# V and wq through GpSimd's DMA queue, and tile 3 of each head transposed by DMA instead of by TensorE

## The chip, the cores and the metric

The kernel runs on one core of a Trainium2 chip. The metric is device time in microseconds (us) of one launch; lower is better. The time before is the median of three runs, and one further execution was recorded by the hardware profiler. The engines are named as in the profile: PE is TensorE (PEld its weight loads), DVE is VectorE, ACT is ScalarE, POOL is GpSimd, SP is SyncE, which only issues DMAs here.

## What is computed

A transformer block: an adaptive layer norm, multi-head attention of 2048 queries against a cached K and V (32 heads of 128, no mask), an output projection, and then a token-shift mixer with an MLP. The change touches the attention alone.

```python
h = _layernorm(x) * (1 + ca) + sa            # x: 1 x 2048 x 640; sa, ca, ... from c and w_mod
q = (h @ wq).reshape(B, Sq, 32, 128).transpose(0, 2, 1, 3)
scores = einsum('bhqd,bhkd->bhqk', q, k_cache) * 128 ** (-0.5)
p = softmax(scores, axis=-1)
o = einsum('bhqk,bhkd->bhqd', p, v_cache)    # k_cache, v_cache: 1 x 32 x 2048 x 128
x = x + ga * (o.transpose(0, 2, 1, 3).reshape(B, Sq, 4096) @ wo)
...                                          # layer norm, mixer and MLP: not touched
```

## The kernel before

**Order of the work.** The program is written as one list of operations for each engine. A small planner (`Prog`) gives each operation the semaphore waits that its reads and writes need; the order on each engine is the order in which the operations are added. A DMA belongs to the queue of the engine that issues it, and waits there like any other operation.

**Attention, step by step.** The loop of line 516 runs over steps s. Step s handles tile j = s % 16 (128 queries) of head h = s // 16, so a head has 16 steps. In each step:

- PE makes the scores of the tile, 128 x 2048 (`qk`, L286), in two halves in PSUM (`Sps`).
- DVE copies each half to SBUF as `negS`, scaled by a negative factor, and takes its minimum in the same instruction (L559). `negS` has three buffers.
- POOL joins the two minima to one (`nm`, L569), and ACT makes the exponentials from `negS` and `nm` (L572) in bf16 into `Pb`, a ring of 8 tiles (`RPB`). So the exponential of tile s writes the place of tile s - 8.
- The tile is transposed, so that keys lie on the partitions: from `Pb` to `PTs`, a ring of 12 tiles. For most tiles a DMA does this on SP's queue (`transpose`, L222), for two neighbouring tiles in one DMA where both go that way. For the tiles in `PE_TILES`, 3 and 10 of each head, PE transposes sixteen 128 x 128 blocks to PSUM three and four steps later (`t_piece`, L253), and ACT (L262) or DVE (L264) copies each half of eight blocks to `PTs` (`t_evac`). DVE copies one half of tile 3 (`by_dve`); ACT copies the other half and both of tile 10.
- PE multiplies the transposed tile of 8 to 11 steps earlier with V (`pv`, L299), ACT copies the result of two tiles to `Of` (L550), and POOL divides by the row sums (L440, L447) and writes four tiles at once to a scratch tensor in DRAM, by a DMA on POOL's own queue (L454).

So with tiles 3 and 10 left out, a head's transposes on SP's queue are the pairs 0-1, 4-5, 6-7, 8-9, 12-13 and 14-15, and tiles 2 and 11 alone: eight DMAs for 14 tiles.

**Loads inside the loop.** All on SP's queue, one head or two ahead, double buffered by head: K of the next head, itself a DMA transpose from DRAM (`load_k`, L205), after step 2; the columns of wq for the head after the next (`load_wq`, L209, 160 KB), after step 6; V of the next head (`load_v`, L214, 512 KB in runs of 256 bytes), after step 12. The projection of the next head's queries is cut into 20 pieces (`q_piece`, L237), which PE runs between the other matmuls in the half steps that `QPIECE` names; it keeps clear of the half steps in which a tile of `PE_TILES` is transposed, since both use the same two PSUM banks. ACT copies each finished 512 columns (L244).

After the last step, the scratch tensor is read back transposed, and the projection, the mixer and the MLP follow.

Of the kernel before, what the change touches and what calls it, by code (L numbers as in the profile page):

```python
# [115 lines left out]
def bass_adaLN_cond__mha_block_cached__mixer_s_mlp__prompt_kernel(  # L116
# [7 lines left out]
    NQT = SQ // 128  # L124
# [13 lines left out]
    with ExitStack() as es:  # L138
# [11 lines left out]
        if True:  # L150
            with ExitStack() as es1:
                sb1 = lambda name, shape, dt: es1.enter_context(nc.sbuf_tensor(name, shape, dt))
                RPB, RPT = 8, 12
                PVD, PVE = 11, 8
                PE_TILES = (3, 10)
                US = KT * (SQ + 4)
                sb1("pad", [128, 32], F32)
                ring = sb1("ring", [128, RPB + RPT, SK], BF16)
# [16 lines left out]
                Vaug = kv[:, o1:o2].rearrange("p (b k d) -> p b k d", b=2, k=NKT)  # L175
                wq = kv[:, o2:o3].rearrange("p (b k d) -> p b k d", b=2, k=KT)
# [24 lines left out]
                G = Prog(nc, es1, "a")  # L201
# [2 lines left out]
                    hb = h % 2  # L204
                    G.dma("sync", lambda e: e.dma_start_transpose(KTs[:, hb], A_k_cache[0, h]), ("k", hb), w=[("KT", hb)])  # L205

                def load_wq(h):
                    hb = h % 2
                    G.dma("sync", lambda e: e.dma_start(wq[:, hb], A_wq[:, h * 128:(h + 1) * 128].rearrange("(k p) d -> p k d", p=128)),  # L209
                          ("wq", hb), w=[("wq", hb)])  # L210

                def load_v(h):
                    hb = h % 2
                    G.dma("sync", lambda e: e.dma_start(Vaug[:, hb, :, 0:128], A_v_cache[0, h].rearrange("(t p) d -> p t d", p=128)),  # L214
                          ("v", hb), w=[("V", hb)])

                assert RPB % 2 == 0 and RPT % 2 == 0 and NQT % 2 == 0
                is_pe = lambda g: g % NQT in PE_TILES

# [14 lines left out]
                def q_piece(h, cc, q):  # L234
                    hb = h % 2
                    jb = bank(("q", h, cc))
                    G.op("tensor", lambda t: t.matmul(JB[jb], wq[:, hb, q, :], hT[:, q, cc * 512:(cc + 1) * 512],  # L237
                                                      start=(q == 0), stop=(q == KT - 1)),
                         r=[("wq", hb), ("hT", cc, q)], w=[("J", jb)])
# [23 lines left out]
                    else:  # L263
                        G.op("vector", lambda v: v.tensor_copy(dst, src), r=[("J", jb)], w=[("PT", g % RPT, r)])  # L264

                by_dve = lambda g, r: r == 1 and g % NQT == PE_TILES[0]

                taken = [u for j in PE_TILES for u in range(2 * (j + 3), 2 * (j + 5))]
                QPIECE = {}
# [62 lines left out]
                if H > 1:  # L332
# [8 lines left out]
                     r=["id0"], w=["ident"])  # L341
# [3 lines left out]
                for k in range(KT):  # L345
                    G.op("gpsimd", lambda g, k=k: g.tensor_scalar(out=s_bc[:, k, :], in0=ones_f, scalar1=c_f[:, k:k + 1],
                                                                  scalar2=1.0, op0=ALU.mult, op1=ALU.mult),
                         r=["onesf", "cf"] + WRK, w=[("sbc", k)])
# [52 lines left out]
                def q_head0(cc):  # L401
                    for q in range(KT):
                        q_piece(0, cc, q)
                    q_evac(0, cc)
# [22 lines left out]
                def mod_rows(i):  # L427
                    n0, n1 = MROW[i]
                    bank = PO[:, (i % 2) * 512:(i % 2) * 512 + n1 - n0]

                    def f(t):
                        for k in range(KT):
                            ins = t.matmul(bank, s_bc[:, k, :], wmodr[:, k, n0:n1], start=(k == 0), stop=(k == KT - 1))
                        return ins
                    G.op("tensor", f, r=[("sbc", k) for k in range(KT)] + [("wm", 1)] + WRK, w=[("O", i % 2)])
                    G.op("scalar", lambda a: a.copy(mod_bc[:, n0:n1], bank), r=[("O", i % 2)], w=[("mod", i)])
# [70 lines left out]
                for g in range(NG):  # L507
                    d = max(PVE, min(PVD, PVE + (NG - 12 - g) // 2))
# [7 lines left out]
                for s in range(at[-1] + LAG + 1):  # L516
                    h, j = divmod(s, NQT)
                    pvs = PVS.get(s, [])
                    evacs = []
                    if s <= 2:  # L520
                        for i in ((0,), (1, 2), range(3, len(MROW)))[s]:
                            mod_rows(i)
                    if s == 3:
                        G.op("gpsimd", lambda g: g.tensor_scalar(
                            out=mod_bc[:, 2 * D:3 * D], in0=mod_bc[:, 2 * D:3 * D], scalar1=1.0, scalar2=1.0, op0=ALU.add, op1=ALU.mult),
                            r=[("mod", i) for i in range(len(MROW))], w=["mod"])
                    for half in range(2):
                        if s < NG:
                            qk(s, half)
                        for g_ in pvs:  # L530
                            if len(pvs) == 1:
                                pv(g_, half)
                            elif g_ == pvs[half]:
                                pv(g_, 0)
                                pv(g_, 1)
                        if s == 0 and half == 1:
                            q_head0(NQC - 1)
                        if h + 1 < H and 2 * j + half in QPIECE:
                            cc, q = QPIECE[2 * j + half]
                            q_piece(h + 1, cc, q)  # L540
                            if q == KT - 1:
                                evacs.append((q_evac, h + 1, cc))
                        for r in range(2):
                            g = s - 3 - r
                            if 0 <= g < NG and is_pe(g):
                                t_piece(g, r, half)
                                if half == 1:
                                    evacs.append((t_evac, g, r))
                    for p in [g_ // 2 for g_ in pvs if g_ % 2 == 1]:
                        G.op("scalar", lambda a, p=p: a.copy(  # L550
                            Of[:, p % 4].rearrange("p z d -> p (z d)")[:, 0:259], PO[:, (p % 2) * 512:(p % 2) * 512 + 259]),
                            r=[("O", p % 2)], w=[("Of", p % 4)])
                    for fn, x, y in evacs:
                        if fn is q_evac or not by_dve(x, y):
                            fn(x, y)
                    for half in range(2):
                        if s < NG:
                            r8 = s % 8
                            G.op("vector", lambda v, half=half, s=s, r8=r8: v.tensor_scalar(  # L559
                                out=negS[:, s % 3, half * 1024:(half + 1) * 1024],  # L560
                                in0=Sps[:, half * 1024:(half + 1) * 1024],
                                scalar1=-SCALE, scalar2=None, op0=ALU.mult, op1=ALU.min,
                                accum_out=(nm0 if half == 0 else nm1)[:, r8:r8 + 1]),
                                r=[("S", half)], w=[("negS", s % 3), ("nmh", half, r8)])
                    for fn, x, y in evacs:
                        if fn is t_evac and by_dve(x, y):
                            fn(x, y)
                    if s < NG:
                        G.op("gpsimd", lambda g, r8=r8: g.tensor_scalar(  # L569
                            out=nm[:, r8:r8 + 1], in0=nm0[:, r8:r8 + 1], scalar1=nm1[:, r8:r8 + 1], scalar2=None, op0=ALU.min),  # L570
                            r=[("nmh", 0, r8), ("nmh", 1, r8)], w=[("nm", r8)])
                        G.op("scalar", lambda a, s=s, r8=r8: a.activation(  # L572
                            Pb[:, s % RPB, :], negS[:, s % 3, :], ACT.Exp, bias=nm[:, r8:r8 + 1], scale=-1.0),
                            r=[("negS", s % 3), ("nm", r8)], w=[("Pb", s % RPB)])
                        if not is_pe(s):
                            if s % 2 == 1 and not is_pe(s - 1):
                                transpose(s - 1, 2)
                            elif s % 2 == 1 or is_pe(s + 1):
                                transpose(s, 1)
                        if j == 2 and h >= 1 and h + 1 < H:  # L580
                            load_k(h + 1)
                        if j == 6 and h + 2 < H:
                            load_wq(h + 2)
                        if j == PVD + 1 and h + 1 < H:
                            load_v(h + 1)
                    for g_ in NORMS.get(s, []):
                        gr, z = divmod(g_, 4)
                        if z == 0:
                            rcp(gr)
                        norm(gr, z)  # L590
                    if s == OT0:
                        load_ot(0)
                        for cc in range(NQC):
                            load_xt(cc)
                    if s == OT0 + 1:
                        load_ot(1)
# [98 lines left out]
                for n in range(KT):  # L695
                    lst = []
                    p = 0
                    while p < 128:
# [8 lines left out]
                        p = pe_  # L707
# [136 lines left out]
```

## Time and profile before

| | |
|---|---|
| Three runs | 1612.88, 1617.95 and 1618.99 us, median 1617.95 us |
| The profiled execution | 1604.1 us, of which its span, from the first to the last instruction, 1602.3 us |
| Granted TensorE clock over the span | 0.993 |
| Attention loop, 37.8 to 1255 us of the span (1217.2 us) | PE busy 1147.1 us, DVE 1192.1, ACT 1194.8, POOL 551.5; DMA moved 240 GB/s |
| The rest, 1255 to 1602.3 us (347.3 us) | PE busy 326.6 us, DVE 173.5, ACT 78.4, POOL 68.5; DMA moved 86 GB/s |
| L559, DVE's scaling with minimum | 1024 times, 1.220 us each |
| L572, ACT's exponentials | 512 times, 2.029 us each |
| L262, ACT's copies of transposed halves | 96 times, 1.034 to 1.042 us each |
| L264, DVE's copies of transposed halves | 32 times, 0.686 us each |
| L253, PE's transposes of blocks | 1024 times, 0.218 us each |
| L222, DMA transposes issued by SP | 256 times, SP's issue 1.63 to 7.63 us, median 4.36; landed 7.1 us after issue in the median |
| L214, loads of V | 32 times, SP's issue 0.58 us in the median; landed after 5.2 us |
| L209, loads of wq | 32 times, SP's issue 0.58 us in the median; landed after 3.6 us |
| L454, results to the scratch tensor, POOL's queue | 128 times, 128 KB each, POOL's issue 0.81 us; landed after 4.5 us |

Busy times are unions of an engine's instructions; a duration of one is longer than the distance between the starts of two in a row where the engine overlaps them. An issue on SP's queue lasts until its descriptors are handed over, and is not a busy time of an engine; the landing is when the last part of the data has arrived. The DMA share of a stretch is the time that packets took on the 16 DMA engines; packets overlap, so it can pass 1, and the bytes moved tell more.

### The profile page before, as it was taken

How to read it: one execution, taken by the hardware profiler on the slowest of the kernel's cores; microseconds unless marked ns; L12 is line 12 of the kernel's file. 1: busy time of each engine (PE TensorE's matmuls, PEld its weight loads, DVE VectorE, ACT ScalarE, POOL GpSimd, SP SyncE). 2: the span in 40 equal slices, each digit the busy share in tenths (PEclk: the TensorE clock that was granted, in tenths of full speed). 3: DMA queues.
4: the chain of work that ended last, by engine and by line, in shares of the span. 5: the costliest groups of instructions: out<-in, count | busy, mean ns of one | idle time of the engine just before them, and what ended most of it. 6: DMA issues, size and time to landing. Idle time of an engine off the chain costs nothing.

```text
span 1602.3 us, 34804 instructions
## 1 busy us (share of the span) xinstructions
PE 1492.6 (93%) x13978; PEld 963.0 (60%) x14231; DVE 1392.5 (87%) x2460; ACT 1288.2 (80%) x1145; POOL 622.8 (39%) x1394
## 2 busy tenths in 40 slices
PE   5799999999999999999999999999999799999998
PEld 3466666666666666666666666666666555545444
DVE  6999999999999999999999999999999266666424
ACT  4999999999999999999999999999999300055330
POOL 0144444444444444444444444444444423322000
PEclk9999999999999999999999999999999899999999
DMA  9999999999999999999999999999999994530000
GB/s 305 229 230 239 238 243 237 253 241 240 237 237 233 239 237 237 239 239 247 243 250 246 250 239 235 246 228 239 236 244 244 241 196 106 106 111 1 17 17 34
DMA packets 1167730, 333.62 MB, mean 208 GB/s; under 512 B 1148304, under 2 KB 1161552, under 8 KB 1167568
## 3 DMA queue, kind: packets, MB, share of 16 engines
q1 hardware_dynamic: 1161424, 314.59, 98.3%
q0 software_dynamic: 6144, 16.79, 3.3%
q8 instruction: 112, 1.84, 0.5%
q14 instruction: 50, 0.41, 0.1%
HBM read 43.48 MB, written 19.40 MB: 39 GB/s over the span
## 4 chain that ended last, share of the span: by engine, by line
DVE 30%; ACT 24%; PE 20%; DMA 15%; issue 10%; POOL 0%; SPq 0%; ACTq 0%; DVEq 0%
DVE negS L559 27%; ACT ring L572 19%; DMA ring<-ring 13%; PE Sps L631 8%; PE Sps L772 4%; PE Oaug L756 2%; PE QPp L756 2%; ACT ring L262 2%; ACT Of L550 2%; PE Sps L741 1%; ACT kv L244 1%; DMA ring<-in_A_x_dram 1%; DVE ring L364 1%; DMA negS<-o_scratch 1%; PE Sps L286 1%
## 5 line engine op out<-in xcount | busy, mean ns | idle before, releaser
L559 DVE TENSOR_SCALAR_CACHE_REDUCE negS<-Sps 128x1024 f32<-128x1024 f32 x1024 | 1177.2, 1220 | 22.2 <-PE Sps L286 12.5
L572 ACT ACTIVATE ring<-negS,small 128x2048 bf16<-128x2048 f32 x512 | 1011.4, 2029 | 21.9 <-DMA ring<-ring 15.7
L299 PEld LDWEIGHTS PTp<-kv,ring 128*128 128x128 bf16 x8192 | 560.0, 98 | 245.0 <-DMA ring<-ring 6.7
L286 PE MATMUL Sps<-kv 128*128 128x512 bf16 x1949 | 596.3, 383 | 62.8 <-DVE negS L559 42.9
L299 PE MATMUL PTp<-kv,ring 128*128 128x129 bf16 x8192 | 645.6, 221 | 6.5 <-DMA ring<-ring 5.6
L569 POOL TENSOR_SCALAR small<-small 128x1 f32<-128x1 f32 x512 | 145.8, 285 | 621.5 <-DVE negS L559 621.4
L286 PEld LDWEIGHTS Sps<-kv 128*128 128x128 bf16 x2048 | 124.5, 97 | 187.2 <-DVE negS L559 158.0
L447 POOL TENSOR_SCALAR On<-Of,small 128x128 bf16<-128x128 f32 x512 | 189.8, 371 | 13.0
L669 ACT COPY kv<-PTp 128x640 bf16<-128x640 bf16 x32 | 22.0, 692 | 155.0 <-PE PTp L666 154.9
L440 POOL TENSOR_TENSOR small<-Of,small 128x4 f32<-128x4 f32 x128 | 133.2, 1040 | 6.3 <-ACT Of L550 6.2
L454 POOL DMA_DIRECT2D o_scratch<-On x128 | 103.1, 806 | 40.8 <-POOL On L447 37.2
L237 PE MATMUL Oaug<-hTx,kv 128*128 128x512 bf16 x265 | 101.2, 387 | 7.9 <-ACT ring L262 4.2
L550 ACT COPY Of<-PTp 128x259 f32<-128x259 f32 x256 | 99.5, 389 | 10.5 <-PE PTp L299 10.5
L237 PE MATMUL QPp<-hTx,kv 128*128 128x512 bf16 x259 | 97.5, 381 | 2.5 <-ACT hTx L391 1.8
L559 DVE DVE_READ_ACCUMULATOR negS<-Sps 128x1 f32 x1024 | 85.4, 83 | 0.0
L612 POOL TENSOR_SCALAR On<-On 128x1 f32<-128x1 f32 x48 | 24.3, 507 | 152.9 <-DVE On L621 152.9
L639 DVE TENSOR_TENSOR ring<-Sps,mod_bc 128x640 f32<-128x640 f32 x16 | 13.2, 825 | 77.0 <-PE Sps L631 77.0
L631 PE MATMUL Sps<-wo,hTx 128*128 128x128 bf16 (+1 forms) x504 | 71.8, 304 | 5.0 <-DMA hTx<-o_scratch 4.7
L776 DVE TENSOR_TENSOR ring<-Sps,ring 128x640 f32<-128x640 f32 x16 | 13.2, 825 | 66.2 <-PE Sps L772 66.2
L631 PE MATMUL Sps<-wo,negS 128*128 128x128 bf16 (+1 forms) x504 | 69.1, 298 | 1.3 <-DMA negS<-o_scratch 0.9
L262 ACT COPY ring<-Oaug 128x1024 bf16<-128x1024 bf16 x64 | 66.2, 1034 | 0.0
L631 PEld LDWEIGHTS Sps<-wo,hTx 128*128 128x128 bf16 x512 | 40.2, 99 | 36.9 <-DMA hTx<-o_scratch 4.5
(82 smaller groups left out, 1011.2 us busy)
## 6 DMA issues: line engine op xcount, KB each, us to landing
kv<-in_A_v_cache_dram SPq DMA_DIRECT2D x32, 512.0 KB, 5.2
o_scratch<-On POOLq DMA_DIRECT2D x128, 128.0 KB, 4.5
ring<-in_A_x_dram SPq DMA_DIRECT2D x8, 640.0 KB, 4.9
kv<-in_A_wq_dram SPq DMA_DIRECT2D x32, 160.0 KB, 3.6
wo<-in_A_wo_dram SPq DMA_DIRECT2D x1, 5120.0 KB, 16.4
ring<-ring SPq DMA_TRANSPOSE x256, 7.1
ring<-in_w_mod_dram SPq DMA_DIRECT2D x1, 3200.0 KB, 13.6
out_dram<-wo SPq DMA_DIRECT2D x16, 160.0 KB, 1.8
```

Source lines behind the costliest of these rows:

```text
L237: G.op("tensor", lambda t: t.matmul(JB[jb], wq[:, hb, q, :], hT[:, q, cc * 512:(cc + 1) * 512], start=(q == 0), stop=(q == KT - 1)), r=[(" ...
L262: G.op("scalar", lambda a: a.copy(dst, src), r=[("J", jb)], w=[("PT", g % RPT, r)])
L286: ins = t.matmul(Sps[:, col:col + 512], QT[:, hb, j * 128:(j + 1) * 128], KTs[:, hb, col:col + 512], start=True, stop=True)
L299: ins = t.matmul(ob[:, 0:129], PTs[:, b, kt, :], Vaug[:, hb, kt, 0:129], start=(kt == 0), stop=(kt == NKT - 1))
L440: G.op("gpsimd", lambda g: g.tensor_tensor(out=rl[:, 4 * b:4 * b + 4], in0=Of[:].rearrange("p a z d -> p (a z) d")[:, 4 * b:4 * b + 4, 128 ...
L447: G.op("gpsimd", lambda g: g.tensor_scalar(out=On[:, b, z, :], in0=Of[:, 2 * b + z // 2, z % 2, 0:128], scalar1=rl[:, 4 * b + z:4 * b + z ...
L454: G.dma("gpsimd", lambda e: e.dma_start(o_scr[jj // 2:jj // 2 + 2, :, hh].rearrange("a p z d -> p a (z d)"), On[:, b].rearrange("p (a z) d ...
L550: G.op("scalar", lambda a, p=p: a.copy(Of[:, p % 4].rearrange("p z d -> p (z d)")[:, 0:259], PO[:, (p % 2) * 512:(p % 2) * 512 + 259]), r= ...
L559: G.op("vector", lambda v, half=half, s=s, r8=r8: v.tensor_scalar(out=negS[:, s % 3, half * 1024:(half + 1) * 1024], in0=Sps[:, half * 102 ...
L569: G.op("gpsimd", lambda g, r8=r8: g.tensor_scalar(out=nm[:, r8:r8 + 1], in0=nm0[:, r8:r8 + 1], scalar1=nm1[:, r8:r8 + 1], scalar2=None, op ...
L572: G.op("scalar", lambda a, s=s, r8=r8: a.activation(Pb[:, s % RPB, :], negS[:, s % 3, :], ACT.Exp, bias=nm[:, r8:r8 + 1], scale=-1.0), r=[ ...
L631: ins = t.matmul(YB[b][:, c0:c0 + cw], OTj[pr % 2][:, 2 * hh + z, :], wo[:, hh, c0:c0 + cw], start=(hh == 0), stop=(hh == H - 1))
```

## The change

`PE_TILES` becomes `(10,)`. Tile 3 is then no longer transposed by PE, and neither ACT nor DVE copies it; it joins tile 2 in one DMA transpose of two tiles on SP's queue. A head's transposes on that queue are still eight, now for 15 tiles. `by_dve` is always false: both halves of tile 10 stay with ACT, as before, and DVE copies none. `QPIECE` now has to keep clear of tile 10's half steps alone, so the 20 pieces fall on half steps 0 to 19 (before: 0 to 9 and 16 to 25).

Inside the loop the loads of wq and of V are issued on POOL's queue, at the same places of the program: behind L569 of step 6 and of step 12, and ahead of the normalization that POOL does in that step. The loads ahead of the loop (wq of heads 0 and 1, V of head 0) and all loads of K stay on SP's queue.

```diff
-                PE_TILES = (3, 10)
+                PE_TILES = (10,)
...
-                def load_wq(h):
+                def load_wq(h, q="sync"):
                     hb = h % 2
-                    G.dma("sync", lambda e: e.dma_start(wq[:, hb], A_wq[:, h * 128:(h + 1) * 128].rearrange("(k p) d -> p k d", p=128)),
-                          ("wq", hb), w=[("wq", hb)])
-
-                def load_v(h):
+                    G.dma(q, lambda e: e.dma_start(wq[:, hb], A_wq[:, h * 128:(h + 1) * 128].rearrange("(k p) d -> p k d", p=128)),
+                          ("wq", hb, q), w=[("wq", hb)])
+
+                def load_v(h, q="sync"):
                     hb = h % 2
-                    G.dma("sync", lambda e: e.dma_start(Vaug[:, hb, :, 0:128], A_v_cache[0, h].rearrange("(t p) d -> p t d", p=128)),
-                          ("v", hb), w=[("V", hb)])
+                    G.dma(q, lambda e: e.dma_start(Vaug[:, hb, :, 0:128], A_v_cache[0, h].rearrange("(t p) d -> p t d", p=128)),
+                          ("v", hb, q), w=[("V", hb)])
...
-                by_dve = lambda g, r: r == 1 and g % NQT == PE_TILES[0]
+                by_dve = lambda g, r: False
...
                         if j == 6 and h + 2 < H:
-                            load_wq(h + 2)
+                            load_wq(h + 2, "gpsimd")
                         if j == PVD + 1 and h + 1 < H:
-                            load_v(h + 1)
+                            load_v(h + 1, "gpsimd")
```

## The prediction

> **What bounds the kernel now.** First the page's busy times and DMA queues.
>
> ```profile
> PE 1492.6 (93%) x13978; PEld 963.0 (60%) x14231; DVE 1392.5 (87%) x2460; ACT 1288.2 (80%) x1145; POOL 622.8 (39%) x1394
> ...
> DMA  9999999999999999999999999999999994530000
> ...
> q1 hardware_dynamic: 1161424, 314.59, 98.3%
> q0 software_dynamic: 6144, 16.79, 3.3%
> ```
>
> In the loop (slices 2 to 32) PE, DVE, ACT and the DMAs all stand at 9. q1 is SP's queue, q0 POOL's. The table by stretches tells DVE and ACT apart from the rest (PE, PEld, DVE, ACT, POOL busy; clock; DMA share; GB/s):
>
> ```profile
> 120.00:320.00 200.00, 192.36 (x1969) 130.32 (x2003) 200.00 (x351) 200.00 (x168) 94.02 (x215) 1.00 1.21 242
> ...
> 520.00:720.00 200.00, 187.00 (x1908) 127.49 (x1942) 194.60 (x340) 194.76 (x163) 90.38 (x209) 1.00 1.24 238
> ```
>
> Early in the loop DVE and ACT never pause. There a head lasts 37.2 us (first L572 of heads 1 to 9, each 37.22 us after the last). That is DVE's work: 32 L559 start 1.144 us apart in the timeline, 36.6 us, and one L264 adds 0.6. Later both lose 5 us in 200, and heads last 37.0 to 39.6 us. The chain of waits in that part names the cause, and the list of waits the same:
>
> ```profile
> 533.09 9.63 DMA ring<-ring
> ...
> 542.80 1.03 ACT ring L572
> 543.83 8.12 DMA ring<-ring
> ...
> 552.03 1.81 ACT ring L572
> ```
>
> ```profile
> ACT ring L572 <- DMA ring<-ring: 15.7, 26, 1.7
> ```
>
> An exponential may not overwrite its place in `Pb` until the DMA has transposed the tile of eight steps before. Now SP's timeline over one head (start, duration, count at the end):
>
> ```profile
> 551.61 2.01 SPq L205 DMA_TRANSPOSE kv<-in_A_k_cache_dram  x1
> 553.66 4.58 SPq L222 DMA_TRANSPOSE ring<-ring  x1
> 558.29 0.59 SPq L209 DMA_DIRECT2D kv<-in_A_wq_dram  x1
> 558.92 11.00 SPq L222 DMA_TRANSPOSE ring<-ring  x3
> 569.96 0.58 SPq L214 DMA_DIRECT2D kv<-in_A_v_cache_dram  x1
> 570.59 19.46 SPq L222 DMA_TRANSPOSE ring<-ring  x4
> 590.10 2.48 SPq L205 DMA_TRANSPOSE kv<-in_A_k_cache_dram  x1
> ```
>
> Each issue starts 0.04 us after the one before: SP's queue never rests. It doesn't wait for ACT either: between 78 and 1216 us (heads 1 to 31) a transpose of tiles 4-5 is issued after its exponentials are done by 1.5 us in head 1, 5.1 in head 4, 7 to 8 in heads 9 to 16. The queue falls behind by 0.6 us a head until the ring of eight is full, and then sets the pace. Its issue times, means of 28 heads between 150 and 1200 us: pairs 0-1, 4-5, 6-7, 8-9, 14-15 take 4.53, 4.54, 4.78, 4.58, 4.49 us; pair 12-13, behind V, 6.27; tiles 2 and 11 alone 2.65 and 2.21; K 2.24, wq 0.59, V 0.58; eleven gaps 0.5. Sum 38.0 us a head. So three limits lie close together: the DMA stream 38.0 us, DVE 37.2, ACT some 37.5 (194.8 busy in 200 us, of a head of 38.5).
>
> **What is removed.** A head of DVE's loses L264, 0.6 us: floor 36.6. ACT's loses one L262, 1.0 us: floor 36.5. PE's loses sixteen L253, four groups of 0.39 us, 1.55 us, from an engine that waits for DVE (158.0 us at L286). None of this is gain while the DMA stream is the longest; it lowers the floor under it, by at most 38.0 - 36.6 = 1.4 us a head. The projection's pieces and ACT's L244 only move.
>
> **What SP's queue loses.** V: its issue with the gap 0.63 us, and the delay of the pair behind it, 6.27 - 4.58 = 1.69; 2.3 together. wq: 0.63 and 4.78 - 4.54 = 0.24, so 0.9. Together 3.2 us a head.
>
> **What it gains.** Tile 2 alone becomes pair 2-3: 4.55 instead of 2.43 (mean of the two single tiles), +2.1 us; at least +1.8, the time of 512 KB at 289 GB/s, the stretch 561 to 564 us in which transposes run undisturbed; at most 4.55 - 2.21 = +2.3. I take 2.0. K of the next head now goes ahead of this pair, whose DMA starts a step later; tile 2 already waits 8.2 us for its issue, so the step is covered.
>
> So SP's queue by itself would need 38.0 - 3.2 + 2.0 = 36.8 us.
>
> **What V and wq cost on POOL's queue.** The trace of before shows none there. Its nearest row is L454, 128 KB four times a head. In windows of 1 to 3 us around its packets:
>
> ```profile
> 561.00:564.00 3.00, 2.85 (x37) 2.24 (x37) 3.00 (x7) 3.00 (x4) 0.62 (x2) 1.00 1.27 289
> 559.00:560.00 1.00, 1.00 (x15) 0.75 (x13) 1.00 (x3) 1.00 (x1) 0.56 (x2) 1.00 0.85 222
> 588.00:590.00 2.00, 2.00 (x23) 1.27 (x21) 2.00 (x5) 1.63 (x2) 0.64 (x2) 1.00 1.27 36
> ```
>
> The first is undisturbed; L454's packets fall at 559.3 us, and just ahead of 588, where the stream then all but stops for two microseconds while its last packet is out. A fit of the distances between landings of the transposes (on tiles, K, wq, V and L454's packets) gives 1.0 us for one L454. Bounds for the 672 KB of V and wq: **from below 0**, if they fit into the stalls that the stream has anyway (38.0 us carry some 31 us of data at 289 GB/s); **from above 5.3 us**, L454's 1.0 us for each 128 KB. Between lie 2.4 us (688 KB in decimal units at 289 GB/s) and 3.2 us, what the same bytes cost now. I take **3.2**, since the same runs of 256 bytes pass the same 16 DMA engines.
>
> The Trainium skill has a rule against the change: "DMA: Bandwidth & Descriptors", section "Issuing engines are not separate DMA queues", says that transfers of SP and POOL run on the same 16 DMA engines, and issuing from both saves only the issuing time. By it the sum below would be +0.7 us a head; that is a rival.
>
> **POOL.** L454 holds POOL 0.81 us for 256 runs. V has 2048 runs, wq 640: between 0.8 us each and 6.4 and 2.0 us by runs. Behind V on POOL stand that step's L447 (0.37) and L569 of step 13, for which the exponential waits; it is due 2.29 us after the last L569 and is used 1.4 us after its end. So up to 3 us are hidden; 6.4 would idle ACT 3.4 us a head. Then ACT needs 36.5 + 3.4 = 39.9 us, still within a head of 40.0, and the ring covers the moment. V and wq wait for nothing: PE has read the old buffers at step 10 and in the head before. They are needed 15 and 10 steps later, 35 and 24 us, against landings of 5.2 and 3.6 us.
>
> **Sum.** 36.8 + 3.2 = 40.0 us a head against 38.0, **+2.0 us**. Head 0 has idle DMA time, so 31 heads: +62 us. The 347 us after the loop stay. The profiled execution's 1602.3 us of span become 1664, its 1604.1 us 1666; the median of the runs shown lies 13.9 us higher (0.9%), so 1617.95 + 62 = **1680 us**.
>
> **Rivals.**
>
> *The loads cost only bytes.* V and wq keep their DMA time, and the stream saves 2 x 0.63 us of issue: -1.26 + 2.0 = +0.7 us a head, +23 us, 1641; with 2.4 us for the loads, 36.8 + 2.4 = 39.2, +37, 1655. For it: V is read, where L454 writes, and what follows a write may not follow a read. Against: SP's issues wait for the DMA engines rather than these for SP, so issue time saved is not stream time saved. This is the skill's rule.
>
> *POOL's packets stop the stream as L454's do.* 36.8 + 5.3 = 42.1, +4.1 us a head, +127 us, 1745. For it: the stall at 588. Against: much of an L454's price may be per transfer and not per byte, and there are two more transfers, not five.
>
> *Faster: the loads fill the stalls.* V and wq use time in which the transposes stand still. Then the stream needs 36.8 us, about DVE's floor, and a head lasts 36.8: -1.2 x 31 = -37, 1581. It decides if the loads cost less than 1.2 us a head (where 36.8 + cost equals 38.0), and POOL is held less than about 4.5 us. For it: 7 us a head of stalls. Against: stalls come mostly beside other transfers, so the loads bring stalls of their own, and 1.2 us is half the time of their bytes.
>
> *The change doesn't do what it says:* no; the planner adds no wait that would put the loads back.
>
> **How the numbers follow.** Chances: forecast (loads at 2.5 to 4.2 us) 0.42, from +1.3 to +3.0 us a head, 1658 to 1711; bytes only, 1626 to 1658, 0.18; as L454, over 1711, 0.13; within 0.5% of 1618 (1610 to 1626, about what a measurement here can tell from no change) 0.08; faster 0.19. The range reaches from 1592, which leaves out the better part of the faster case, to 1735: about 1 in 10 is left out on each side. Faster 0.19, same 0.08, slower 0.73.
>
> **What would show it.** DVE and ACT busy per head down by 0.6 and 1.0 us, but more waits of L572 for the transposes, several times 15.7 us, from head 2 or 3 on. SP's issues still back to back, pair 12-13 down to some 4.6 us, pair 2-3 at 4.5, and pairs near V's packets longer. POOL's instruction for V between 0.8 and 6.4 us. Wrong: SP's queue with pauses and heads of 36.6 to 37 us, or L572 waiting for L569 more than for the DMA.

## The result, and the profile after

The changed kernel takes 1724.89 us (median of four runs, 1716.73 to 1741.2) against 1618.47 us before: a ratio of 1.0676, 95% interval 1.0593 to 1.0758, +106 us by the medians. The forecast was slower, +62 us. The profiled execution took 1723.53 us, its span 1721.7. Runs more than 1.5% above the fastest of the same kernel are left out of the ratios below: two of four with wq back on SP's queue, one of four with wq at step 8.

The page's busy times and DMA queues, after:

```profile
PE 1502.4 (87%) x13474; PEld 943.6 (55%) x13719; DVE 1380.2 (80%) x2428; ACT 1264.8 (73%) x1113; POOL 692.5 (40%) x1455
...
DMA  9999999999999999999999999999999996630000
...
q1 hardware_dynamic: 1143296, 310.19, 93.3%
q0 software_dynamic: 12528, 37.96, 9.4%
```

DVE and ACT have less to do in more time; the DMAs are as full as before, and POOL's queue q0 now carries 38 MB instead of 17. The same two stretches as before (PE, PEld, DVE, ACT, POOL busy; clock; DMA share; GB/s):

```profile
120.00:320.00 200.00, 175.26 (x1707) 114.53 (x1738) 179.61 (x314) 175.90 (x147) 97.51 (x208) 0.99 1.21 233
520.00:720.00 200.00, 169.06 (x1624) 111.22 (x1655) 171.66 (x297) 170.31 (x142) 91.80 (x195) 0.97 1.21 230
```

DVE and ACT, which before never paused early in the loop, now idle 20 to 30 us in 200, and the DMAs move 230 to 233 GB/s, where 238 to 242 were moved before. The waits and a piece of the chain say on whom:

```profile
ACT ring L572 <- DMA ring<-ring: 153.0, 75, 9.0
...
DVE negS L559 <- ACT ring L572: 138.9, 88, 9.8
```

```profile
601.18 8.04 DMA ring<-ring
...
609.30 1.38 ACT ring L572
610.68 9.80 DMA ring<-ring
...
620.56 2.06 ACT ring L572 x2
```

The exponentials wait ten times as long for the transposes as before (15.7 us), and DVE waits for the exponentials (8.7 us before). PE's granted clock is lower over the span (0.976 against 0.993), but that is not what costs: an L299 takes 223 ns instead of 221, and DVE waits for the scores of L286 14.5 us in all instead of 12.5. SP's queue still never rests:

```profile
552.45 2.05 SPq L205 DMA_TRANSPOSE kv<-in_A_k_cache_dram  x1
554.55 39.62 SPq L222 DMA_TRANSPOSE ring<-ring  x8
594.21 2.45 SPq L205 DMA_TRANSPOSE kv<-in_A_k_cache_dram  x1
```

One K and eight transposes fill the time from 552.45 to 594.21 us, 41.8 us for a head. The mean issue times (25 heads between 150 and 1200 us) tell where they grew: pairs 0-1, 2-3, 4-5, 12-13 and 14-15 take 4.42, 4.80, 4.63, 4.44 and 4.94 us, much as a pair did before, but 6-7 and 8-9, beside V, take 6.75 and 6.10 instead of 4.78 and 4.58, and K 3.32 instead of 2.24. With tile 11's 2.53 and nine gaps of 0.05 the sum is 42.4 us a head, against 38.0.

Three stretches show what V does there, the first just before V's packets. V was issued by POOL at 566.0 us; most of its packets ran from 572 to 574. The last row is from another head, whose V was issued at 687.89:

```profile
570.90:571.90 1.00, 0.93 (x11) 0.55 (x9) 1.00 (x3) 1.00 (x2) 0.62 (x2) 1.00 1.27 290
572.00:574.00 2.00, 1.84 (x19) 1.10 (x17) 1.86 (x5) 2.00 (x3) 1.31 (x3) 1.00 1.12 260
...
691.50:697.00 5.50, 3.59 (x38) 2.52 (x38) 3.71 (x7) 5.38 (x5) 1.91 (x5) 1.00 1.25 109
```

In the first, transposes run undisturbed at 290 GB/s. In the second nearly everything that moves is V: of SP's queue 28 packets began, where 568 in each half microsecond are the full pace. In the third both queues crawl, 109 GB/s together, and ACT pays with its longest wait:

```profile
706.61 3.90 ACT L572 ACTIVATE ring<-negS,small 128x2048 bf16<-128x2048 f32 x2 [9.01 <-DMA ring<-ring]
```

### The profile page after: what moved, and what is told of

Same layout as the page of the kernel before. It is cut to its first block, busy times and chain, and to the rows that moved or that the text cites. A ratio compares the mean times of both kernels' runs of the same rounds, so it can differ in the third digit from the quotient of the medians.

```text
span 1721.7 us, 33785 instructions
## 1 busy us (share of the span) xinstructions
PE 1502.4 (87%) x13474; PEld 943.6 (55%) x13719; DVE 1380.2 (80%) x2428; ACT 1264.8 (73%) x1113; POOL 692.5 (40%) x1455
## 4 chain that ended last, share of the span: by engine, by line
DMA 33%; ACT 30%; PE 19%; DVE 9%; issue 7%; POOL 1%; SPq 0%; ACTq 0%; DVEq 0%; POOLq 0%
DMA ring<-ring 31%; ACT ring L572 24%; DVE negS L559 8%; PE Sps L631 7%; PE Sps L772 4%; ACT kv L244 2%; ACT Of L550 2%; PE Oaug L756 2%; PE QPp L756 2%; PE Sps L741 1%; ACT ring L262 1%; DMA negS<-o_scratch 1%; DMA ring<-in_A_x_dram 1%; DVE ring L364 1%; PE Sps L286 1%
## 5 line engine op out<-in xcount | busy, mean ns | idle before, releaser
L572 ACT ACTIVATE ring<-negS,small 128x2048 bf16<-128x2048 f32 x512 | 1013.4, 2011 | 164.0 <-DMA ring<-ring 153.0
L299 PEld LDWEIGHTS PTp<-kv,ring 128*128 128x128 bf16 x8192 | 567.3, 99 | 309.8 <-DMA ring<-ring 73.9
L299 PE MATMUL PTp<-kv,ring 128*128 128x129 bf16 x8192 | 656.3, 223 | 57.4 <-DMA ring<-ring 57.1
L286 PE MATMUL Sps<-kv 128*128 128x512 bf16 x1963 | 608.5, 389 | 110.2 <-DVE negS L559 87.7
L569 POOL TENSOR_SCALAR small<-small 128x1 f32<-128x1 f32 x512 | 147.9, 289 | 665.4 <-DVE negS L559 663.4
L286 PEld LDWEIGHTS Sps<-kv 128*128 128x128 bf16 x2048 | 130.4, 98 | 253.2 <-DVE negS L559 196.9
L447 POOL TENSOR_SCALAR On<-Of,small 128x128 bf16<-128x128 f32 x512 | 191.9, 375 | 15.7
L454 POOL DMA_DIRECT2D o_scratch<-On x128 | 101.1, 790 | 37.9 <-POOL On L447 37.9
L550 ACT COPY Of<-PTp 128x259 f32<-128x259 f32 x256 | 95.3, 372 | 11.1 <-PE PTp L299 11.1
L631 PEld LDWEIGHTS Sps<-wo,negS 128*128 128x128 bf16 x512 | 39.6, 98 | 31.2 <-DMA negS<-o_scratch 0.9
```

The costliest lines, as they stand in the source:

```text
L286: ins = t.matmul(Sps[:, col:col + 512], QT[:, hb, j * 128:(j + 1) * 128], KTs[:, hb, col:col + 512], start=True, stop=True)
L299: ins = t.matmul(ob[:, 0:129], PTs[:, b, kt, :], Vaug[:, hb, kt, 0:129], start=(kt == 0), stop=(kt == NKT - 1))
L447: G.op("gpsimd", lambda g: g.tensor_scalar(out=On[:, b, z, :], in0=Of[:, 2 * b + z // 2, z % 2, 0:128], scalar1=rl[:, 4 * b + z:4 * b + z ...
L454: G.dma("gpsimd", lambda e: e.dma_start(o_scr[jj // 2:jj // 2 + 2, :, hh].rearrange("a p z d -> p a (z d)"), On[:, b].rearrange("p (a z) d ...
L550: G.op("scalar", lambda a, p=p: a.copy(Of[:, p % 4].rearrange("p z d -> p (z d)")[:, 0:259], PO[:, (p % 2) * 512:(p % 2) * 512 + 259]), r= ...
L569: G.op("gpsimd", lambda g, r8=r8: g.tensor_scalar(out=nm[:, r8:r8 + 1], in0=nm0[:, r8:r8 + 1], scalar1=nm1[:, r8:r8 + 1], scalar2=None, op ...
```

## The experiments

Each kernel ran beside the kernel before on the same chip. Ratios are to that kernel, with 95% intervals. In the diffs, `-` is the changed kernel where the text says so, else the kernel before; `...` stands for lines left out.

| kernel | tile 3 | V | wq | time, us | ratio |
|---|---|---|---|---|---|
| loads moved | TensorE | POOL | POOL | 1628.08 | 1.0053 (1.0027 to 1.0078) |
| tile moved | DMA | SP | SP | 1681.96 | 1.0378 (1.0352 to 1.0405) |
| V moved | TensorE | POOL | SP | 1629.07 | 1.0062 (1.0031 to 1.0092) |
| wq moved | TensorE | SP | POOL | 1616.46 | 0.9961 (0.9935 to 0.9987) |
| wq back | DMA | POOL | SP | 1772.11 and 1793.36 | 1.1003 (1.0915 to 1.1091) |
| V back | DMA | SP | POOL | 1669.93 | 1.0313 (1.0275 to 1.0352) |
| the change | DMA | POOL | POOL | 1724.89 | 1.0676 (1.0593 to 1.0758) |

### The two parts alone

The loads alone, with tile 3 on TensorE and its copy on DVE as before:

```diff
-                            load_wq(h + 2)
+                            load_wq(h + 2, "gpsimd")
...
-                            load_v(h + 1)
+                            load_v(h + 1, "gpsimd")
```

> The kernel before with only the loads of V and wq moved to POOL's queue; tile 3 stays with TensorE. Theory A (POOL's packets stop the transposes; by the fit of landing distances in the changed kernel V costs 3.7 us a head there and wq 1.5, against 2.2 and 1.1 on SP's queue, so +1.9 us): heads of some 39.8 us, +1.9 x 31 = +59 us, 1670 to 1685. Theory B (the loads cost the same on either queue and the extra transposed tile cost more than 2.0 us): within 8 us of the kernel before. Theory C (bytes only, the issue time is saved): 10 to 25 us faster.

Measured: +0.5%, some 8 us. Neither +59 nor a gain: near theory B's figure. Beside tile 3 on TensorE, V and wq cost almost the same on either queue: +8 / 31 = +0.3 us a head.

The tile alone:

```diff
-                PE_TILES = (3, 10)
+                PE_TILES = (10,)
...
-                by_dve = lambda g, r: r == 1 and g % NQT == PE_TILES[0]
+                by_dve = lambda g, r: False
```

> The kernel before with only tile 3 moved from TensorE to the DMA; V and wq stay on SP's queue. Theory A: +1.8 to 2.0 us a head, +56 to +62 us, 1672 to 1682. Theory B (the tile is what costs): +3.4 us a head, some +105 us, 1723. If the two parts disturb each other, this and the run with the loads alone stay well below their sum of +106 us.

Measured: +61 us, 2.0 us for each of 31 heads, as theory A had it; theory B falls. The wait of the exponentials for the transposes, in the list of waits of this kernel:

```profile
ACT ring L572 <- DMA ring<-ring: 107.7, 89, 3.6
```

The sum of the parts is +69 us, and the change costs +106: some 37 us come from both together, with some 14 us of doubt either way, by the intervals. The longest wait is telling: 3.6 us here, 9.0 with the change.

V alone:

```diff
-                            load_v(h + 1)
+                            load_v(h + 1, "gpsimd")
```

> The kernel before with only V on POOL's queue; wq on SP's, tile 3 with TensorE. Theory A by bytes: V makes 3.7 - 2.2 = +1.5 of the +1.9 us a head of both loads, +46 us, 1664. If the price is one for each transfer and not for its bytes, V makes half of what both loads make, some +30 us, 1648.

Measured: +0.6%, the same as both loads; neither figure was met. The theory by bytes falls for this setting, and wq seems to cost nothing. The profiled execution has one bad case all the same: V issued at 145.2 us landed 18.2 us later. It is one of three runs of ten at 1641 to 1643 us; the other seven took 1623 to 1631.

### The writes of the result on SP's queue

```diff
-                    G.dma("gpsimd", lambda e: e.dma_start(
+                    G.dma("sync", lambda e: e.dma_start(
                         o_scr[jj // 2:jj // 2 + 2, :, hh].rearrange("a p z d -> p a (z d)"),
```

> The kernel before with the writes of the attention result (L454, 128 KB, four a head) on SP's queue instead of POOL's. Theory A (what is on another queue than the transposes stops them): each write costs some 0.5 us instead of 0.9 to 1.0, the stream falls from 38.0 to about 36.2 us a head, and DVE's 37.2 us set the pace: up to 25 us faster, 1593 to 1600. Rival (the writes stop the transposes because they go to DRAM, on whatever queue): no change, or slower where SP waits for POOL's last division with the transposes behind it.

Measured: 1646.2 us, ratio 1.0153 (1.0128 to 1.0177), 1.5% slower. Its list of waits says why:

```profile
POOL On L447 <- DMA o_scratch<-On: 145.3, 34, 27.3
...
ACT ring L572 <- POOL small L569: 58.7, 39, 3.9
```

The write now stands behind the transposes, so POOL waits for its two buffers `On`, and L569 with the exponentials behind it. Whether the writes got cheaper for the stream is not shown: what that is worth is hidden behind these waits.

### Which load, beside the tile

From here `-` is the changed kernel.

```diff
-                            load_wq(h + 2, "gpsimd")
+                            load_wq(h + 2)
```

> The changed kernel with wq back on SP's queue; V stays on POOL's. The loads alone made the kernel before slower by 0.5%, the tile alone by 3.8%; together 6.8%. Open is which load costs 1.2 us a head more beside the extra tile. Theory V (V on POOL's queue, later into a fuller stream, is what grew: 2.4 to 3.9 us a head): little change, 1710 to 1725. Theory wq (wq is issued on POOL when SP, some 8 us behind, issues K, and both meet L454's write of step 6): 1690 to 1700.

```diff
-                            load_v(h + 1, "gpsimd")
+                            load_v(h + 1)
```

> The changed kernel with V back on SP's queue; wq stays on POOL's. Theory V: near the kernel with the tile alone, 1682 to 1692. Theory wq: 1710 to 1725. If each gives back half, the two loads disturb each other.

```diff
-                        if j == 6 and h + 2 < H:
+                        if j == 8 and h + 2 < H:
```

> The changed kernel with wq issued on POOL's queue behind step 8 instead of step 6, two steps away from L454's write of step 6 and from K. Theory wq: 15 to 35 us faster than the changed kernel, 1690 to 1710, with K landing after some 5 us instead of 6.7. Theory V: within 10 us of 1725.

```diff
-                        if j == PVD + 1 and h + 1 < H:
+                        if j == PVD + 1 and h + 1 < min(H, 2):
```

> The changed kernel without the loads of V from head 2 on: heads 2 to 31 use the V of heads 0 and 1, so the output is not the reference's. It prices V on POOL's queue. Theory V: 3.9 us a head gone in 30 heads, -117 us, some 1608. Theory wq: V costs what it costs on SP's queue, 2.3 us, -70 us, some 1655.

Measured: with V back on SP's queue the ratio is 1.0313, 12 us *faster* than with the tile alone and below both expectations. With wq issued at step 8 it is 1.0685 (1.064 to 1.073), no difference from the change. Without the loads of V from head 2 on it is 0.9979 (0.9951 to 1.0007). So theory wq falls, and V is the load that costs: on POOL's queue (1.0676 - 0.9979) x 1621 / 30 = 3.8 us a head, on SP's (1.0313 - 0.9979) x 1621 / 30 = 1.8, both a little low, since without V some heads run at DVE's floor of 36.6 us. With wq back on SP's queue and V left on POOL's the ratio was 1.1003, far outside either expectation: the kernel loses another 53 us when wq leaves POOL's queue. Its profiled execution took longer still, 1805.4 us; in it V landed 12.0 us after its issue in the median, at most 23.6 (between 150 and 1250 us). So the trouble is again V's; why it grows is not explained.

How long V takes and what stands still meanwhile differs between the settings. From the sources' views, the landings of V after its issue (least, median, most, us), first the changed kernel, then the loads moved with tile 3 on TensorE, then V back on SP's queue:

```profile
DMA to landing us min/median/max: 5.8/9.1/16.9
```

```profile
DMA to landing us min/median/max: 5.1/7.6/9.9
```

```profile
DMA to landing us min/median/max: 4.5/5.1/6.7
```

Between V's issue and its landing, tenths of a microsecond in which SP's queue began fewer than 34 packets (114 is the full pace) add up to

```
                                 mean us   longest us   V's counted
changed kernel                     5.0        11.6          27
loads moved, tile 3 on TensorE     3.5         5.2          28
V back on SP's queue               0.8         2.1          29
```

The last row is not V's whole price in line: by the runs V costs 1.8 us a head there. The 1.5 us between the first two rows, times 31, is 46 us, enough for the 37 us by which the change exceeds its parts, and it sits in a tail. Of the 27, twenty lie between 2.6 and 4.9 us and seven between 6.0 and 11.6. POOL's issue is not at fault: its instruction for V takes 1.23 to 1.26 us each time.

The same count over whole heads (3 to 26, all transfers) is 6.3 us a head in the kernel before and 9.5 with the loads moved, 3.2 more; with the tile moved it is 6.8 and with the change 11.4, 4.5 more. So the same two loads bring more standstill beside tile 3's DMA transpose.

### Another queue, another step, smaller pieces, and wq alone

```diff
-                            load_v(h + 1, "gpsimd")
+                            load_v(h + 1, "scalar")
```

> The changed kernel with V issued on ACT's queue, behind step 12's exponential, instead of POOL's. So far, in the changed kernel: V on POOL's queue 1725 us, on SP's 1670, no V 1618; in its profile the transposes stand still 5.0 us for each V, up to 11.6, in stretches where packets of both queues crawl. Theory 1 (any second queue interrupts the transposes): 1705 to 1740. Theory 2 (POOL's queue does it): the cost of V as on SP's queue, 1665 to 1680, with some 0.6 us a head more on ACT, which is not the limit.

Measured: 1686.6 us, 1.04 (1.0357 to 1.0442), between the theories. Moving V from SP's queue to ACT's costs 14 to 17 us, to POOL's 55 to 59. V's landings in this kernel:

```profile
DMA to landing us min/median/max: 5.5/6.3/8.8
```

The transposes stand still 2.9 us for each V, at most 4.6. So ACT's queue interrupts them too, and POOL's does so longer.

```diff
-                        if j == PVD + 1 and h + 1 < H:
+                        if j == PVD and h + 1 < H:
```

> The changed kernel with V issued on POOL's queue behind step 11 instead of 12, so that the next L454 comes three steps later instead of two. Theory: V grows long because L454 (issued 5.3 us behind it) falls into its transfer: 1680 to 1705, and fewer standstills over 5 us. Rival: the overlap has nothing to do with it (with tile 3 on TensorE the two overlap as well, at 3.5 us for each V): 1715 to 1740.

Measured: 1704.31 us, 1.0496 (1.0446 to 1.0546), 20 us less than the change. Standstills are 4.4 us in the mean. Where the next L454 was issued within 7.6 us of V (14 of 27) the mean is 5.3 and five are over 5; where it came later, 3.3, and none is. That speaks for a part of the overlap. But with tile 3 on TensorE an L454 was issued before each V had landed, at 3.5 us of standstill, so it isn't the whole.

```diff
-                def load_v(h, q="sync"):
+                def load_v(h, i):
                     hb = h % 2
-                    G.dma(q, lambda e: e.dma_start(Vaug[:, hb, :, 0:128], A_v_cache[0, h].rearrange("(t p) d -> p t d", p=128)),
-                          ("v", hb, q), w=[("V", hb)])
+                    G.dma("gpsimd", lambda e: e.dma_start(Vaug[:, hb, 4 * i:4 * i + 4, 0:128],
+                          A_v_cache[0, h, i * 512:(i + 1) * 512].rearrange("(t p) d -> p t d", p=128)),
+                          ("v", hb, i), w=[("V", hb, i)])
...
-                        if j == PVD + 1 and h + 1 < H:
-                            load_v(h + 1, "gpsimd")
+                        if j > PVD and h + 1 < H:
+                            load_v(h + 1, j - PVD - 1)
```

> The changed kernel with V in four transfers of 128 KB on POOL's queue, behind steps 12, 13, 14 and 15. Theory: what costs is the long burst of one transfer, which shuts the transposes out; four short ones cost what four L454 cost, 3.6 to 4.0 us a head without the long tail: 1700 to 1715. If short pieces slip in between the transposes: 1670 to 1680. If every transfer on POOL's queue brings its own interruption on top of its bytes: over 1735.

Measured: 1691.29 us, 1.0419 (1.0373 to 1.0465): 34 us faster than in one transfer, and faster than the theory of the long burst said (its 1700 to 1715 counted four times an L454's price). In this kernel's DMA issues:

```profile
o_scratch<-On POOLq DMA_DIRECT2D x128, 128.0 KB, 5.5
kv<-in_A_v_cache_dram POOLq DMA_DIRECT2D x124, 128.0 KB, 5.5
```

A quarter of V lands as an L454 does. So four short transfers a head cost less than one long one.

wq alone on POOL's queue, against the kernel before:

```diff
-                            load_wq(h + 2)
+                            load_wq(h + 2, "gpsimd")
```

> The kernel before with only wq on POOL's queue; V on SP's, tile 3 with TensorE. Beside the tile moved to the DMA, wq on POOL's queue was 12 us faster than on SP's (1670 against 1682). If that holds here too, the stream falls from 38.0 to some 37.6 us a head: 6 to 12 us faster than the kernel before. If DVE's 37.2 us and the waits around it leave no room, or the price of wq is the same on both queues: no difference.

Measured: 1616.46 us, 0.9961 (0.9935 to 0.9987), 5 to 6 us faster than the kernel before: clear of no difference by little, at the low end of the 6 to 12 us expected. No kernel here that loads every V was faster.

## Why the prediction was right, and where its size was off

The direction, the bound and the tile's term came out as forecast. The price of the loads was too small, and the reason given for it, their bytes, was the wrong one. The 1725 us lie above the band of the central case (1658 to 1711), in that of the rival *as L454*, which was given 0.13. That they still fall inside the stated range was partly luck: nothing in the sum stands for what the tile and the loads do to each other, some 37 us.

- **The bound**: right. The DMA stream on SP's queue set the pace and still does; its issues stay back to back, and the work taken from PE, DVE and ACT (DVE 12 us less busy in all, ACT 23) is worth nothing.
- **The extra tile, +2.0 us a head**: right. Alone it cost 61 / 31 = 2.0.
- **V and wq off SP's queue, -3.2**: right where it can be seen. Pair 12-13 fell from 6.27 to 4.44 us, against some 4.6 forecast.
- **Their price on POOL's queue, 3.2 ("since the same runs of 256 bytes pass the same 16 DMA engines")**: this is the term that was mis-sized. The change costs 106 / 31 = 3.4 us a head, so the loads cost 3.4 - 2.0 + 3.2 = 4.6, nearer to the upper bound of 5.3. With tile 3 on TensorE it nearly holds (3.2 + 0.3 = 3.5). wq was if anything cheaper there than on SP's queue; V was dearer. The reason given, bytes through the same engines, left out what the view of L454 had shown: packets of another queue shut the transposes out. The upper bound had it, by bytes; it was taken as less likely.
- **POOL**: V holds it 1.26 us, wq 0.98, near the lower bound of 0.8 and far from 6.4. L572 waits for L569 6.1 us in all, 5.8 before.

The rivals: *bytes only* falls, since V costs more on ACT's or POOL's queue than on SP's, though its issue leaves SP. The rule of the Trainium skill ("DMA: Bandwidth & Descriptors", section "Issuing engines are not separate DMA queues") is that DMAs issued by SP, ACT or POOL run on the same 16 DMA engines, and issuing from several saves issue time alone. The runs agree that another queue brings no bandwidth (230 to 233 GB/s after, 238 to 242 before), but moving V was not neutral either, +14 to 17 us on ACT's queue and +55 to 59 on POOL's. *As L454* was nearest to the truth in mechanism and size (1745 us), though its price by bytes is not shown: what was dear is V beside tile 3's transpose. *Faster* falls with the loads alone: they did not fill the stalls.

What stays open: why V's transfer on POOL's queue sometimes turns into a crawl of 6 to 12 us of standstill, why it does so often beside tile 3's transpose (seven of 27) and rarely without it (once in the profile of V alone moved, 11.5 us, and never in that of both loads moved), and why putting wq back on SP's queue makes it worse. The step of wq is not it; an L454 within V's transfer seems to be a part.

## What to carry to other kernels

Where a stream of DMA transposes sets the pace, another load's price need not be its bytes: look at what the transposes do while it passes, and price a move to another queue by the nearest transfer that already runs there. Parts of a change that share a saturated resource need not add up; run each alone and both together. And leave a long transfer in line (1670 us here), or, if it must go on another queue, try it in pieces (1691 against 1725).

## What the runs showed of the hardware that was not expected

While V's packets of POOL's queue ran (572 to 574 us), SP's transposes began 28 packets, where the pace before and after is 568 in each half microsecond: in that stretch the two queues took turns in blocks. In the bad case (691.5 to 697 us) packets of both ran side by side and together moved 109 GB/s for 5.5 us, with single packets of V lasting up to 2.4 us instead of the usual 0.31. And POOL's instruction for a DMA hardly grows with the number of runs: 0.79 us for 256, 0.98 for 640, 1.26 for 2048.
